# Key slots 128 bytes longer, and the third pair's stacked weights loaded and split half a pair sooner

## The chip, the core and the metric

The kernel runs on one core of one Trainium2 chip. The metric is the device time of one execution in microseconds (us). Before the change it is 1113.81 us, the median of three runs (1112.98 to 1114.1).

## What is computed

A transformer block in float32 on one sequence of 2048 rows of 576 numbers: a layer norm, then windowed attention (32 heads of 18 numbers, eight keys at a distance of two rows) and, in parallel, a squared-ReLU layer with 4608 hidden units. Cut to what matters:

```python
def _A_ref(x, wqkv, wo):
    q, k, v = split(x @ wqkv)
    idx = pos[:, None] - arange(8)[None] * 2
    logits = einsum("bhsd,bhswd->bhsw", q, k[idx]) * 18 ** -0.5
    attn = softmax(where(idx >= 0, logits, -1e9))
    return einsum("bhsw,bhswd->bhsd", attn, v[idx]) @ wo

def _B_ref(x, w1, b1, w2, b2):
    r = relu(x @ w1 + b1)
    return (r * r) @ w2 + b2

xn = layernorm(x)
return x + _A_ref(xn, ...) + _B_ref(xn, ...)
```

## The kernel before

**Tiling.** The 2048 rows are four blocks of 512 (`b` = 0 to 3), taken in two halves (`s` = 0: blocks 0 and 1, `s` = 1: blocks 2 and 3). The 576 input rows of a product are four chunks of 128 and a rest of 64. The 4608 hidden units are 36 tiles of 128, taken two at a time as 18 pairs `p`. Every float32 operand is split into a high part that TensorE takes in one pass (ScalarE, ACT, rounds it) and a low part (VectorE, DVE, subtracts); a product is high by high plus the two mixed terms.

**One pair** (`ffn_pair`) multiplies two hidden tiles with two blocks by seven products of Strassen's kind (`T1`, `T3`, `B11`, `T2`, `B22`, `B21`, `T4`) instead of eight. A `product` is six matmuls of 128x128 by 128x512, and `work(0)` to `work(3)` put seven matmuls each of the second layer (line 533) between them. TensorE (PE) takes them in the order B11, T1, work(0), T2, work(1), T3, B21, work(2), B22, T4, work(3). In the first half the rest of 64 rows costs eight further matmuls for each pair (`left`, line 633), which makes 7 x 6 + 8 + 28 = 78. In the second half, from pair 2 on, the rest is **stacked**: one further matmul for each product takes high and low parts of the rest together, its weights from `LW[p % 2]` (a part of a tile named `w1r`) and its moving operand from `ST[...]` (tiles `x40`, `x41`, `x4d` and the second `w1r` tile). That makes 7 x 7 + 28 = 77.

**Where the stacked weights come from.** `load_left_weights(p)` (line 584) fetches 256 KB on the SP queue into the raw tile `LR["w"]`, named `mb`, of which there is one. `left_weight_sums` makes the Strassen sums in it (three DVE instructions). `left_weight_hi(p)` rounds it into `LW[p % 2]` on ACT (line 593). `left_weight_lo(p)` subtracts on DVE, and then issues the load for `p + 1` into the same raw tile. In the second half, pair 0 has the end of the attention projection of block 1 as its filler; pair 1 makes the stacks of the rest (`stack_sums`, `stack_hi`, `stack_lo`; tiles `kv` and `w1r`), and in its later part loads and splits the weights of pair 2, the third pair. From pair 2 on each pair prepares the weights of the next one (`ready`).

**Order.** Nothing is reordered: each engine and each DMA queue takes its instructions as the code issues them. DVE and ACT also carry the attention of later blocks, in pieces that `side(k)` issues one after the other. The raw weights of the second layer (`w2r`) are loaded on the same SP queue, each load as soon as DVE has taken the low part of the tile three before it.

**Memory.** Tiles of one name share slots in a pool, laid out one after the other in each partition. A key or value tile is 18 x 144 numbers, 10368 bytes, in three slots named `kv`; behind them lie `w1r`, `w2r`, `mb`, `pr`, `lg`, `r4`, `st`, some small tiles, `nm`, `xf`, `mr`, `mrt` and `q`. Ahead of them lie `h`, `X`, `x4`, `w1s`, `S` and `w2s`, from which nearly all matmuls read.

Of the kernel before, what the change touches and what calls it, by code (L numbers as in the profile page):

```python
# [8 lines left out]
F32 = mybir.dt.float32  # L9
# [7 lines left out]
P = 128  # L17
S, D, F = 2048, 576, 4608
# [3 lines left out]
NJ = TB // P  # L22
# [5 lines left out]
CG = HG * DH  # L28
QW = 3 * CG
HALO = (W - 1) * DIL  # L30
NE = HALO + NJ
# [14 lines left out]
def block_kernel(ctx: ExitStack, tc: tile.TileContext, x, xt, wqkv, wo, w1, b1, w2, b2, w1l, out):  # L46
# [3 lines left out]
    sb = ctx.enter_context(tc.tile_pool(name="sb", bufs=1))  # L50
# [6 lines left out]
    ov = out[:DM].rearrange("(c p) (b t) -> b p c t", p=P, b=NB)  # L57
    oe = out[DM:].rearrange("d (b t) -> b d t", b=NB)

    x0 = sb.tile([P, NJ, D], F32, name="kv", bufs=3)  # L60
    w0 = sb.tile([P, NC - 1, QW], F32, name="w1r", bufs=2)
    w4 = sb.tile([P, DE], F32, name="w2r", bufs=3)
    r0 = [w0[:, c] for c in range(NC - 1)] + [w4[:, :QW]]
# [33 lines left out]
    def flat(t, off, parts, n):  # L97
        a = t[0:1, 0:1]
        return bass.AP(tensor=a.tensor, offset=a.offset + off, ap=[parts, [1, n]])
# [4 lines left out]
    def tt(out, a, b, op):  # L104
        return nc.vector.tensor_tensor(out=out, in0=a, in1=b, op=op)  # L105
# [12 lines left out]
    X, x4, SS, xm, xf, mb = {}, {}, {}, {}, {}, {}  # L118
# [26 lines left out]
    def load_rows(b):  # L145
        rows_of[b] = sb.tile([P, NJ, D], F32, name="kv", bufs=3)
        nc.sync.dma_start(rows_of[b], xv[b])
# [194 lines left out]
    loads, landed, queue, free, lane, kept_back = [], {}, [], [0], [nc.sync], [0]  # L342

    def fetch():
        while free[0] > kept_back[0] and loads:
            free[0] -= 1
            kind, b, g = loads.pop(0)
            if kind == "x":
                load_rows(b)
                landed["x", b] = True  # L350
                continue
            t = landed[kind, b, g] = sb.tile([P, NE, CG], F32, name="kv", bufs=3)
            if kind == "k":
                q = landed["q", b, g] = sb.tile([P, NJ, CG], F32, name="q", bufs=2)
                lane[0].dma_start(q.rearrange("p j c -> p (j c)"),
                                  flat(scr["q"][g], (PAD + b * TB) * CG, [NJ * CG, P], NJ * CG))
            lane[0].dma_start(t.rearrange("p e c -> p (e c)"),
                              flat(scr[kind][g], (PAD + b * TB - HALO) * CG, [NJ * CG, P], NE * CG))

    def release():  # L360
        free[0] += 1
        fetch()
# [55 lines left out]
    def side(k, exp=True):  # L418

        while k > 0:  # L420
            if current[0] is None:
                if not queue or queue[0][0] not in landed:
                    return k
                name, make = queue.pop(0)
                current[:] = [make(), None, name]
            if current[1] == "exp" and not exp:
                return k
            try:
                current[1] = next(current[0])
                k -= 1  # L430
            except StopIteration:
                current[0] = None
        return 0
# [107 lines left out]
    ST, LW, LR = {}, {}, {}  # L541
    STACK = {T1: 0, T3: 1, B11: 2, T2: 3, B22: 4, B21: 5, T4: 6}

    def load_left_rows():
        t = LR["a"] = sb.tile([P, 4, TB], F32, name="w1r", bufs=2)
        nc.vector.memset(t[3 * L:], 0.0)
        for g in range(3):
            for k, b in enumerate((2, 3)):
                nc.sync.dma_start(t[g * L:(g + 1) * L, 2 * k:2 * k + 2], xlscr[b].rearrange("(q r) t -> r q t", q=2))

    def stack_sums():
        a, z = LR["a"], LR["s"]
        tt(z[:, 0], a[:, 2], a[:, 3], ALU.add)
        tt(z[:, 2], a[:, 0], a[:, 2], ALU.subtract)
        tt(z[:, 1], z[:, 0], a[:, 0], ALU.subtract)
        tt(z[:, 3], a[:, 1], z[:, 1], ALU.subtract)

    def stack_hi(to, v):
        nc.scalar.activation(to, v, AF.Copy)

    def stack_lo(to, v):
        rows = slice(L, 2 * L)
        tt(to[rows], v[rows], to[rows].bitcast(F32), ALU.subtract)

    def open_stacks():
        t = LR["st"] = sb.tile([P, 4, TB], F32R, name="w1r", bufs=2)
        for i, k in enumerate((B11, B21, T4, T1)):
            ST[k] = t[:, i]

    def one_stack(k, name):  # L570
        ST[k] = mt.tile([P, TB], F32R, name=name)
        stack_hi(ST[k], LR["s"][:, {T2: 1, T3: 2, B22: 3}[k]])

    def one_stack_lo(k):
        stack_lo(ST[k], LR["s"][:, {T2: 1, T3: 2, B22: 3}[k]])

    def open_left_weights():
        t = sb.tile([P, 2, 7, P], F32R, name="w1r", bufs=2)
        LR["w"] = sb.tile([P, 7, P], F32, name="mb")
        LW[0], LW[1] = t[:, 0], t[:, 1]  # L580

    def load_left_weights(p):
        if p < NP:
            nc.sync.dma_start(LR["w"][:, 2:6], w1l[p])

    def left_weight_sums():
        r = LR["w"]
        tt(r[:, 0:2], r[:, 3:5], r[:, 2:4], ALU.subtract)
        tt(r[:, 3], r[:, 4], r[:, 0], ALU.subtract)
        tt(r[:, 6], r[:, 5], r[:, 3], ALU.subtract)  # L590

    def left_weight_hi(p):
        nc.scalar.activation(LW[p % 2], LR["w"], AF.Copy)

    def left_weight_lo(p):
        rows = slice(2 * L, P)
        tt(LW[p % 2][rows], LR["w"][rows], LW[p % 2][rows].bitcast(F32), ALU.subtract)
        load_left_weights(p + 1)
# [4 lines left out]
    def ffn_pair(s, p, work, first=False):  # L603
        b0, b1 = 2 * s, 2 * s + 1
        n = s * NP + p
# [14 lines left out]
        def product(to, slot, a, start=False):  # L620
            mm = [(weight(slot, 0, c), a(0, c)) for c in range(2)]
            for c in range(2):
                mm += [(weight(slot, 1, c), a(0, c)), (weight(slot, 0, c), a(1, c))]
            if stacked:
                mm.append((LW[p % 2][:, STACK[slot]], ST[slot]))
            for i, (l, r) in enumerate(mm):
                nc.tensor.matmul(to, l, r, start=start and i == 0, stop=i == len(mm) - 1, skip_group_check=True)  # L627

        def left(to, f, v):
            if stacked:  # L630
                return
            for k in range(2):
                nc.tensor.matmul(to, weight(LEFT, k, f), v, start=False, stop=k == 1, skip_group_check=True)  # L633
# [35 lines left out]
        if s and p == 2:  # L669
# [3 lines left out]
            one_stack_lo(B22)  # L673
            release()
        if s and p == 1:
            stack_sums()
            open_stacks()
            stack_hi(LR["st"][:, 0:2], LR["a"][:, 0:2])
            stack_hi(ST[T4], LR["a"][:, 3])
# [53 lines left out]
        relu(r0[:, 0], ba, f0)  # L733
        if s and p == 1:
            open_left_weights()
            load_left_weights(2)
            stack_lo(ST[T1], LR["s"][:, 0])
            one_stack(T2, "x40")
        work(2)

        def third():
            product(bc, B22, S4)
            left(bc, 1, x4["d"])
            if s and p == 1:
                one_stack_lo(T2)
                left_weight_sums()
                left_weight_hi(2)
            elif not first:
                side(2)
            tt(r0[:, 1], bc, u[:, 0], ALU.add)  # L750
            relu(r0[:, 1], r0[:, 1], f1)
# [12 lines left out]
        else:  # L764
# [1 line left out]
            h0 = square_hi(r0)  # L766
            square(r0)
            fourth()
        if s and p == 1:
            left_weight_lo(2)  # L770
        side(2, False)
        hs[n] = h0
        prev["r"] = r0, r1, h0
# [310 lines left out]
    def phase_b0():  # L1084
        b = 1
# [119 lines left out]
        def filler(i):  # L1205
            if i < 2:
                quads(1, 1, [len(steps) - 2 + i])
            if i == 1:
                load_left_rows()
                for g in (2, 3):  # L1210
                    offer(2, g)
                for g in range(G):
                    offer(3, g)
            if i == 2:
                xr[b] = [mt.tile([P, NC - 1, TB], F32, name="h", bufs=3)]
                nc.sync.dma_start(xr[b][0], yscr)
                open_y(b)
                o_hi(b, 0), o_hi(b, 1)
                o_lo(b, 0), o_lo(b, 1)
            if i == 2.5:  # L1220
                o_hi(b, 2), o_hi(b, 3)
                chunks(0)
                o_lo(b, 2), o_lo(b, 3)
                chunks(1)
            if i == 3:
                open_left(b)
                nc.sync.dma_start(kept(b, NC - 1), yleft)
                o_hi(b, 4)
                o_lo(b, 4)
                next(prev["finish"])  # L1230
                chunks(2)
                side(1)
                chunks(3)
                w2_hi()
                add(b, o_ops(b, 4), range(NC))
                finish(b, False)
                w2_lo()
# [80 lines left out]
    def open_rows():  # L1318
# [23 lines left out]
            inverse_std(rs[j], ln[0, j][:, 1:2])  # L1342

        def minus_mean(j):
            nm = sb.tile([P, 1], F32, name="nm", bufs=2)
            nc.vector.tensor_scalar(out=nm, in0=ln[0, j][:, 0:1], scalar1=-1.0, scalar2=rs[j], op0=ALU.mult, op1=ALU.mult)
            return nm

# [88 lines left out]
        nm = minus_mean(2)  # L1437
# [19 lines left out]
        nm = minus_mean(3)  # L1457
# [161 lines left out]
```

## Time and profile before

The profiled execution took 1115.46 us, of which 1113.8 us is the span from the first to the last instruction; the rest lies around it.

| of the span of 1113.8 us | busy |
|---|---|
| PE (matmuls) | 1102.4 us, 99% |
| DVE | 912.0 us, 82% |
| ACT | 575.5 us, 52% |
| POOL | 115.2 us, 10% |
| DMA | 258 GB/s mean |

| stage | us from the span's start |
|---|---|
| queries, keys and values of blocks 0 and 1 | 0 to 112 |
| pairs of the first half | 112 to 410 |
| second layer of block 1 | 410 to 547 |
| queries, keys and values of blocks 2 and 3 | 547 to 621 |
| pair 0 of the second half, and the projection of block 1 | 621 to 652 |
| pair 1 | 652 to 670 |
| pairs 2 to 17 | 670 to 957 |
| second layer of block 3, and the end | 957 to 1114 |

Rows of a timeline give start, duration, engine, line, operation, output <- inputs, shape, and in brackets how long the engine was idle before and what ended that. Matmuls overlap, and a row's duration runs to the modelled end of its last one: the pace is read from one row's start to the next one's. Line 105 is a helper that every DVE operation on two tensors goes through, so such rows are told apart by their tiles.

### The profile page before, as it was taken

To read this page: it belongs to the slowest core of one execution; us is meant where nothing else is said; L and a number is where in the kernel's file an instruction comes from. 1 tells how busy PE (TensorE), PEld (TensorE's weight loads), DVE (VectorE), ACT (ScalarE), POOL (GpSimd) and SP (SyncE) were. 2 spreads that over 40 slices of the span, in tenths; PEclk is the share of its full clock that TensorE was granted. 3 is DMA by queue.
4 is the path that set the end of the run, shared out by engine and by line. 5 is a ranking of instruction groups with operands and counts; after the bars stand their busy time and mean duration, and the time that the engine had idled before them with its cause. 6 is when DMAs were issued, how large, how long until landed. Compare 5 with 4: busy or idle time off the path is not lost.

```text
span 1113.8 us, 13890 instructions
## 1 busy us (share of the span) xinstructions
PE 1102.4 (99%) x4950; PEld 926.3 (83%) x4950; DVE 912.0 (82%) x1223; ACT 575.5 (52%) x809; POOL 115.2 (10%) x219
## 2 busy tenths in 40 slices
PE   9999999999999999999999998999999999999998
PEld 7998888888888888888899886888888888888886
DVE  7696979897997979999979488978988788899654
ACT  5435765556566554456344355555555555533342
POOL 4000101020110100100010200202102021001100
PEclk9999999999999999999999999999999999999999
DMA  8957987889799686966855976768686685866762
GB/s 295 337 167 237 338 295 262 293 206 372 250 246 364 250 329 221 337 227 213 277 147 158 335 264 252 276 247 319 216 312 236 263 314 203 311 207 209 277 192 82
DMA packets 100279, 287.83 MB, mean 258 GB/s; under 512 B 13288, under 2 KB 41712, under 8 KB 85488
## 3 DMA queue, kind: packets, MB, share of 16 engines
q1 hardware_dynamic: 65280, 188.15, 49.1%
q0 software_dynamic: 10544, 52.14, 13.0%
q10 hardware_dynamic: 24384, 46.64, 12.3%
q8 instruction: 39, 0.64, 0.2%
q14 instruction: 32, 0.26, 0.1%
HBM read 205.14 MB, written 81.74 MB: 258 GB/s over the span
## 4 chain that ended last, share of the span: by engine, by line
PE 92%; DVE 3%; DMA 2%; ACT 1%; issue 1%; POOL 0%; ACTq 0%; SPq 0%; DVEq 0%; POOLq 0%
PE p L533 46%; PE p L627 31%; PE p L1041 6%; PE p L335 5%; PE p L633 3%; PE p L1045 1%; DMA w1s<-w 1%; DMA mb<-in_w1l 1%; PE p L1399 1%; DVE h L105 0%; DVE w1r L105 0%; DVE pr L105 0%; DVE w1s L105 0%; DVE w2s L105 0%; DMA kv<-in_x 0%
## 5 line engine op out<-in xcount | busy, mean ns | idle before, releaser
L533 PE MATMUL p<-h,w2s 128*128 128x512 f32 x2066 | 493.0, 390 | 0.2 <-ACT h L640 0.2
L533 PEld LDWEIGHTS p<-h,w2s 128*128 128x128 f32 x2066 | 387.9, 188 | 83.3 <-ACT h L640 0.6
L627 PE MATMUL p<-X,w1s 128*128 128x512 f32 x864 | 220.5, 390 | 0.8 <-DVE w1s L105 0.8
L627 PEld LDWEIGHTS p<-X,w1s 128*128 128x128 f32 x864 | 162.2, 188 | 36.0 <-DVE w1s L105 1.2
L506 ACT ACTIVATE w2s<-w2r 128x640 fp32r<-128x640 f32 x164 | 120.2, 735 | 114.9 <-PE p L533 89.2
L627 PE MATMUL p<-S,w1s 128*128 128x512 f32 x648 | 166.7, 393 | 0.6 <-ACT r L688 0.6
L105 DVE TENSOR_TENSOR w2s<-w2r,w2s 128x576 fp32r<-128x576 f32 x164 | 123.4, 754 | 40.5 <-ACT w2s L506 39.7
L627 PEld LDWEIGHTS p<-S,w1s 128*128 128x128 f32 x648 | 122.3, 189 | 27.2 <-ACT r L688 1.4
L412 POOL DMA_DIRECT2D o<-q x128 | 69.3, 607 | 584.4 <-DVE q L105 582.5
L636 ACT ACTIVATE r<-r,b1t 128x512 f32<-128x512 f32 x72 | 52.0, 722 | 124.9 <-DVE r L105 123.8
L384 DVE TENSOR_REDUCE lg<-pr 128x64 f32<-128x1152 f32 x64 | 86.5, 1352 | 1.5
L105 DVE TENSOR_TENSOR pr<-lg,kv 128x1152 f32<-128x1152 f32 x64 | 86.7, 1355 | 1.3
L105 DVE TENSOR_TENSOR pr<-q,kv 128x1152 f32<-128x1152 f32 x64 | 86.6, 1353 | 0.9
L105 DVE TENSOR_TENSOR pr<-pr 128x576 f32<-128x576 f32 (+1 forms) x128 | 77.5, 606 | 3.2
L644 ACT ACTIVATE r<-r 128x1024 f32<-128x1024 f32 x72 | 76.1, 1057 | 1.2
L105 DVE TENSOR_TENSOR h<-r,h 128x1024 fp32r<-128x1024 f32 (+3 forms) x46 | 51.8, 1136 | 26.6 <-ACT r L644 18.5
L105 DVE TENSOR_TENSOR r<-p,r 128x512 f32<-128x512 f32 (+1 forms) x77 | 53.0, 688 | 23.1 <-PE p L627 11.4
L105 DVE TENSOR_TENSOR w1s<-w1r,w1s 128x1024 fp32r<-128x1024 f32 (+1 forms) x42 | 50.3, 1198 | 16.5 <-ACT w1s L474 16.4
L688 ACT ACTIVATE r<-p 128x512 f32<-128x512 f32 x36 | 21.6, 599 | 72.8 <-PE p L627 72.4
L105 DVE TENSOR_TENSOR h<-h 128x1024 fp32r<-128x1024 f32 x36 | 43.9, 1221 | 5.4 <-ACT h L938 5.4
L636 ACT ACTIVATE r<-p,b1t 128x512 f32<-128x512 f32 x72 | 48.3, 672 | 0.0
L533 PE MATMUL p<-w1s,w2s 128*128 128x512 f32 x195 | 44.7, 389 | 0.0
(193 smaller groups left out, 1174.9 us busy)
## 6 DMA issues: line engine op xcount, KB each, us to landing
w2r<-in_w SPq DMA_DIRECT2D x144, 320.0 KB, 3.6
kv<-kvq POOLq DMA_DIRECT2D x29, 1296.0 KB, 9.6
w<-w1s SPq DMA_DIRECT2D x36, 1024.0 KB, 8.9
w1s<-w ACTq DMA_DIRECT2D x34, 1024.0 KB, 7.3
h<-r SPq DMA_DIRECT2D x36, 512.0 KB, 6.6
h<-h SPq DMA_DIRECT2D x36, 512.0 KB, 4.0
w1r<-in_w SPq DMA_DIRECT2D x18, 640.0 KB, 7.6
kvq<-st ACTq DMA_DIRECT2D x48, 216.0 KB, 3.8
```

The costliest lines, as they stand in the source:

```text
L105: return nc.vector.tensor_tensor(out=out, in0=a, in1=b, op=op)
L335: nc.tensor.matmul(p[:, :QW], l, r, start=k == 0, stop=k == len(mm) - 1)
L384: nc.vector.tensor_reduce(out=lg[:, j * HG:(j + 1) * HG].rearrange("p a w -> p w a"), in_=pr.rearrange("p w (a d) -> p w a d", d=DH), axis ...
L412: nc.gpsimd.dma_start(rows[:, i], q[i * L:(i + 1) * L, :, a:z])
L506: nc.scalar.activation(w2s[stream[i]][:, :DE], raw2[i], AF.Copy)
L533: nc.tensor.matmul(yp[b][c], v, a, start=c not in yb[b], stop=c in last and c not in [o[0] for o in ops[i + 1:]], skip_group_check=True)
L627: nc.tensor.matmul(to, l, r, start=start and i == 0, stop=i == len(mm) - 1, skip_group_check=True)
L633: nc.tensor.matmul(to, weight(LEFT, k, f), v, start=False, stop=k == 1, skip_group_check=True)
L636: nc.scalar.activation(to, a, AF.Relu, bias=b1t[:, f:f + 1])
L644: nc.scalar.activation(r, r, AF.Square)
L688: nc.scalar.activation(u[:, 0], bb, AF.Copy)
L1041: nc.tensor.matmul(to, l[:, js], r, start=start and n == 0, stop=n == len(mm) - 1, skip_group_check=True)
```

## The change

There are two parts.

**The load and the split of the third pair's stacked weights.** The raw tile `mb` is opened and its load issued in pair 0's filler, behind the loads of the rest's rows (`load_left_rows`), instead of in pair 1. The sums go ahead of `stack_sums` in pair 1, the high part to where the load was, and the low part behind product B22, with the load for pair 3 right after it.

**Addresses.** Key and value tiles get 32 more float32 at their end (128 bytes), so a slot is 10496 bytes instead of 10368; each of the two slots of `nm` is 32 floats instead of one. What is computed with them is the same. Where tiles start, modulo 256 bytes, in the memory maps of the two programs:

| tiles | before | after |
|---|---|---|
| `h`, `X`, `x40`, `x41`, `x4d`, `w1s`, `S`, `w2s` | 224 | 224 |
| `kv` (three slots) | 224, 96, 224 | 224, 224, 224 |
| `w1r`, `w2r`, `mb`, `pr`, `r4` | 96 | 224 |
| `xf` | 160 | 224 |
| `q` | 192 | 0 |

```diff
-    x0 = sb.tile([P, NJ, D], F32, name="kv", bufs=3)
+    def kv_tile(n):
+        return sb.tile([P, n], F32, name="kv", bufs=3)
+
+    x0 = kv_tile(NJ * D).rearrange("p (j d) -> p j d", d=D)
...
-            t = landed[kind, b, g] = sb.tile([P, NE, CG], F32, name="kv", bufs=3)
+            t = landed[kind, b, g] = kv_tile(NE * CG + 32)[:, :NE * CG].rearrange("p (e c) -> p e c", c=CG)
...
     def open_left_weights():
         t = sb.tile([P, 2, 7, P], F32R, name="w1r", bufs=2)
-        LR["w"] = sb.tile([P, 7, P], F32, name="mb")
         LW[0], LW[1] = t[:, 0], t[:, 1]
...
         if s and p == 1:
+            left_weight_sums()
             stack_sums()
...
             open_left_weights()
-            load_left_weights(2)
+            left_weight_hi(2)
             stack_lo(ST[T1], LR["s"][:, 0])
             one_stack(T2, "x40")
...
             if s and p == 1:
+                left_weight_lo(2)
                 one_stack_lo(T2)
-                left_weight_sums()
-                left_weight_hi(2)
...
-        if s and p == 1:
-            left_weight_lo(2)
         side(2, False)
...
                 load_left_rows()
+                LR["w"] = sb.tile([P, 7, P], F32, name="mb")
+                load_left_weights(2)
...
-            nm = sb.tile([P, 1], F32, name="nm", bufs=2)
+            nm = sb.tile([P, 32], F32, name="nm", bufs=2)[:, :1]
```

On DVE, from the split of a `w2s` tile in pair 1 to the first attention piece (`pr`) behind pair 1, before (`kv<-w1r` and its two neighbours are the stack sums, `mb<-mb` the sums of the stacked weights, `w1r<-mb` their low part, `r<-p,r` additions that free a PSUM bank):

```order
L105 TENSOR_TENSOR kv<-w1r 128x512 x2
L105 TENSOR_TENSOR kv<-kv,w1r 128x512
L105 TENSOR_TENSOR kv<-w1r,kv 128x512
...
L105 TENSOR_TENSOR r_5626<-p_5556,r_5596 128x512
L105 TENSOR_TENSOR w1r<-kv,w1r 32x512
L105 TENSOR_TENSOR x_5644<-kv,x_5644 32x512
L105 TENSOR_TENSOR mb<-mb 128x256
L105 TENSOR_TENSOR mb<-mb 128x128 x2
L105 TENSOR_TENSOR r_5625<-p_5556,r_5596 128x512
L105 TENSOR_TENSOR w1r<-mb,w1r 64x896
L105 TENSOR_TENSOR pr<-q,kv 128x1152
```

and after:

```order
L108 TENSOR_TENSOR mb<-mb 128x256
L108 TENSOR_TENSOR mb<-mb 128x128 x2
L108 TENSOR_TENSOR kv<-w1r 128x512 x2
L108 TENSOR_TENSOR kv<-kv,w1r 128x512
L108 TENSOR_TENSOR kv<-w1r,kv 128x512
...
L108 TENSOR_TENSOR r_5631<-p_5558,r_5601 128x512
L108 TENSOR_TENSOR w1r<-kv,w1r 32x512
L108 TENSOR_TENSOR w1r<-mb,w1r 64x896
L108 TENSOR_TENSOR x_5648<-kv,x_5648 32x512
L108 TENSOR_TENSOR r_5630<-p_5558,r_5601 128x512
L108 TENSOR_TENSOR pr<-q,kv 128x1152
```

The three sums moved ahead of the stack sums, and the low part ahead of the second `r<-p,r`, which no longer has the sums in front of it. On ACT, `w1r<-mb` (line 593) changes places with the copy of one stack that stood ahead of it.

On the SP queue, from the loads of the rest's rows on, before:

```order
L549 DMA w1r<-xl_148 32x2x512
L1216 DMA h<-y_185 128x2048
...
L496 DMA w2r<-in_w 128x640 x2
L584 DMA mb<-in_w1l 128x512 x2
L654 DMA h_168<-r_5626 128x1024
```

and after:

```order
L552 DMA w1r<-xl_148 32x2x512
L586 DMA mb<-in_w1l 128x512
L1218 DMA h<-y_185 128x2048
...
L499 DMA w2r<-in_w 128x640 x2
L586 DMA mb<-in_w1l 128x512
L656 DMA h_168<-r_5631 128x1024
```

The first of two loads of `mb` moved ahead of the load of `h`, past nine loads and four stores; the second stays where it was. PE's and POOL's instructions keep their order.

## The prediction

> **What bounds the kernel now.** I read the page first, its busy times and its chain of waits:
>
> ```profile
> PE 1102.4 (99%) x4950; PEld 926.3 (83%) x4950; DVE 912.0 (82%) x1223; ACT 575.5 (52%) x809; POOL 115.2 (10%) x219
> PE 92%; DVE 3%; DMA 2%; ACT 1%; issue 1%; POOL 0%; ACTq 0%; SPq 0%; DVEq 0%; POOLq 0%
> ```
>
> TensorE sets the end. No matmul is added or removed, so time can come only from PE's waits, from its clock, and from the pace at which matmuls follow each other. The view of waits names the one long wait inside the program:
>
> ```profile
> PE p L627 <- DVE w1r L105: 2.9, 1, 2.9
> ```
>
> The timeline at the border of pairs 1 and 2 shows what led to it, and windows its clock (columns: stretch, length, then busy time of PE, PEld, DVE, ACT, POOL, granted clock, DMA share, GB/s):
>
> ```profile
> 631.47 5.79 SPq L549 DMA_DIRECT2D w1r<-xl  x6
> 657.30 1.28 DVE L105 TENSOR_TENSOR kv<-w1r 128x512 f32<-128x512 f32 x2
> 664.51 0.69 DVE L105 TENSOR_TENSOR r<-p,r 128x512 f32<-128x512 f32 x1
> 664.89 10.48 SPq L584 DMA_DIRECT2D mb<-in_w1l  x2
> 665.24 0.73 ACT L636 ACTIVATE r<-r,b1t 128x512 f32<-128x512 f32 x1 [2.61 <-DVE r L105]
> 665.25 1.23 PEld L627 LDWEIGHTS p<-X,w1s 128*128 128x128 f32 x6 [0.29 <-DVE r L105]
> 670.60 1.52 PE L627 MATMUL p<-X,w1s 128*128 128x512 f32 x6
> 671.78 1.08 DVE L105 TENSOR_TENSOR mb<-mb 128x256 f32<-128x256 f32 x3 [4.01 <-DMA mb<-in_w1l]
> 672.78 0.68 DVE L105 TENSOR_TENSOR r<-p,r 128x512 f32<-128x512 f32 x1
> 672.95 0.95 ACT L593 ACTIVATE w1r<-mb 128x896 fp32r<-128x896 f32 x1 [5.89 <-DVE mb L105]
> 673.93 1.09 DVE L105 TENSOR_TENSOR w1r<-mb,w1r 64x896 fp32r<-64x896 f32 x1 [0.46 <-ACT w1r L593]
> 675.05 1.36 DVE L105 TENSOR_TENSOR pr<-q,kv 128x1152 f32<-128x1152 f32 x1
> 675.07 0.79 PE L627 MATMUL p<-w1r 128*128 128x512 f32 x1 [2.95 <-DVE w1r L105]
> 678.53 1.76 PE L533 MATMUL p<-h,w2s 128*128 128x512 f32 x7
> 682.17 0.42 ACT L393 ACTIVATE lg<-lg 128x256 f32<-128x256 f32 x1 [2.30 <-DVE lg L105]
> 683.76 1.66 PE L627 MATMUL p<-S,w1s 128*128 128x512 f32 x6 [0.28 <-ACT r L688]
> ```
>
> ```profile
> 671.73:675.07 3.34, 0.39 (x2) 0.00 (x1) 2.72 (x6) 2.09 (x3) 0.00 (x0) 0.98 0.00 0
> 675.07:678.53 3.46, 3.46 (x8) 2.75 (x9) 3.43 (x3) 3.40 (x5) 0.54 (x1) 0.52 0.47 148
> ```
>
> The weights arrive at 671.8, DVE sums them, ACT rounds, DVE takes the low part until 675.02, and PE's seventh matmul of pair 2 goes at 675.07. Then the granted clock is 0.52 for 3.46 us.
>
> For the pace I take the chain in order of time, where PE waits for nothing: two pairs of the first half, then pairs of the second.
>
> ```profile
> 146.19 2.72 PE p L627 x12
> 148.91 1.59 PE p L533 x7
> 163.87 2.72 PE p L627 x12
> 701.77 3.20 PE p L627 x14
> 704.97 1.62 PE p L533 x7
> 949.48 3.20 PE p L627 x14
> 957.51 2.54 PE p L533 x11
> ```
>
> 12 matmuls in 2.72 us and 7 in 1.59 are 227 ns each. A pair of the first half takes 163.87 - 146.19 = 17.68 us for 78 matmuls, 226.7 ns each. A pair of the second half takes (949.48 - 701.77) / 14 = 17.69 us for 77, 229.8 ns each: the matmul that stacking saves is given back by pace.
>
> **The load and split: what the wait costs.** At 227 ns, work(0) would start 14 matmuls behind 670.60, at 673.78; it starts at 678.53. The wait and the half clock behind it cost 4.75 us (3.1 us of standing, 1.65 us of slow matmuls). Then T3 would follow behind work(0), T2 and work(1), 21 matmuls behind 678.53, at 683.3. It starts at 683.76, because the copy of T2 stands on ACT behind the exponential, which waits for DVE: 0.45 us, and 0.1 us more at its first matmuls.
>
> **What takes its place.** The load now goes out behind the loads of the rest's rows, at 631.47 + 5.79 = 637.3, and its sums need it at 657.3: hidden. The three sums (1.08 us) go ahead of the stack sums, into a stretch where DVE has no gap:
>
> ```profile
> 652.92:665.20 12.28, 12.28 (x55) 9.96 (x54) 12.12 (x18) 5.14 (x8) 0.00 (x0) 1.00 0.92 309
> ```
>
> Queued behind them are the stack sums, two `w2s` splits, the stack splits and the `r<-p,r` of 664.51, for which PE waits before B22. That wait, 0.29 us on the weight side now, grows by the whole 1.08. A pause of 1.2 us is a third of the one that brought the half clock, so I price no clock for it. In the new order ACT rounds the weights behind its two relus, at about 667.5 to 668.5 (now: relus from 665.24, moved by 1.08). DVE takes the low part (1.09) until 669.6, the stack part until 670.2 and the second `r<-p,r` (0.68) until 670.9. PE wants the weights at 670.60 + 1.08 + 1.36 = 673.0: they are ready 3.4 us before. The added ACT and DVE times there (0.95 and 1.09) lie in gaps of 5.89 and 4.01 us in the rows above.
>
> **What is late next.** DVE's chain to T3 (attention, low part of `h`, sums for pair 3, two stack splits, maximum, exponential on ACT, copy of T2) starts at `pr`, now 675.05, then 670.85: 4.2 us earlier, so T3 may start at 679.56. PE gets there at 683.76 - 4.75 - 0.45 + 1.08 = 679.64. The two nearly tie, and T3's wait goes. The sums for pair 3 need their load, issued at about 669.6, by 674.85.
>
> ```profile
> DMA to landing us min/median/max: 2.6/6.9/11.2
> ```
>
> Of 16 such loads the fastest landed in 2.6 us and the median in 6.9. The engines moved nothing from 671.73 to 675.07, so I take some 3 us and no wait; at 6.9 it would land at 676.5, 1.65 us late. Sum of this part: -4.75 - 0.55 + 1.08 = **-4.2 us**, bounds -2.5 (the late load) and -4.75 (half of the 1.08 absorbed).
>
> **Addresses.** Nothing in the trace shows a 128-byte step by itself, so I look for what differs between matmuls that run at 227 ns and those that do not.
>
> ```profile
> L627 PE MATMUL p<-w1r x64: 393/393/794, 675.1 to 957.1; 128*128 128x512 f32 x64
> L627 PE MATMUL p<-x,w1r x32: 397/397/397, 681.5 to 950.7; 128*128 128x512 f32 x32
> L533 PE MATMUL p<-xf,w2s x9: 394/394/394, 650.6 to 652.5; 128*128 128x512 f32 x9
> L533 PE MATMUL p<-w1s,w2s 128*128 128x512 f32 x195 | 44.7, 389 | 0.0
> ```
>
> Those on `w1r` (weights, or both operands) and those on `xf` show 393 to 397 ns, and all nine of `xf` 394. Their twins on `w1s`, the same operation on the same weights, show 389. `w1r` and `xf` are the tiles of 512-column matmuls that do not start at 224 modulo 256, and after the change they do. Matmuls behind a `w1r` one run slow too: the seven of 704.97 take 1.62 us, not 1.59. If the start is the cause, the second half goes to 226.7 ns: 77 x 3.1 = 0.24 us a pair, over (957.51 - 683.76) / 17.69 = 15.5 pairs 3.7 us, and 0.05 for `xf`. Bounds: 0, and -3.8. It might also be the place far back in the partition, which stays; but 432-column matmuls that read `r4` (short `r` in the rows), further back still, show what those on `h` show (by line and form: busy us, mean ns):
>
> ```profile
> L1041 PE MATMUL p<-h,X 128*128 128x432 f32 x144 | 32.1, 358 | 0.0
> L1041 PE MATMUL p<-r,X 128*128 128x432 f32 x48 | 10.2, 359 | 0.0
> ```
>
> That leaves the start. I take **-3.75 us**.
>
> A rule speaks against this term. The Trainium skill (SBUF — State Buffer, Who interferes with whom) says that PE and ACT never wait on anyone at their ports, and its section on operand start alignment speaks of legality alone. By it the term is 0 and the sum -4.2; no run here shows yet which holds.
>
> For DVE the step costs nothing by these rows: the `kv` slots already start 128 bytes apart modulo 256, and 64 instructions on them agree within 1%.
>
> ```profile
> L105 DVE TENSOR_TENSOR pr<-q,kv x64: 1347/1352/1361, 53.1 to 1014.0; 128x1152 f32<-128x1152 f32 x64
> ```
>
> **Sum.** -4.2 - 3.75 = -7.95 us. The profiled execution took 1115.46 (span 1113.8), which gives 1107.5; the median of the runs, 1113.81, lies 1.65 below it. That is what the half clock cost, so the runs may lack it and gain that much less (again 1107.5), or the difference has nothing to do with it (1105.9). I take **1106.6**, with a range of its own of 1105.3 to 1108.
>
> **Rivals.**
>
> *The addresses change nothing.* Only the wait goes: 1109.6 by the median, 1111.3 with the half clock missing from it, middle 1110.4. For it: matmuls on `h` and `w2s` run slow behind `w1r` although both start at 224. Against: nine equal `xf` rows. This is also what the Trainium skill's SBUF page would have.
>
> *A new wait takes the place of the old.* Pair 3's weights land after 6.9 us, the exponential and T3 come 1.65 us later: 1108.2 with the address term, 1112 without. For it the median landing; against it the idle DMA engines.
>
> *Slower: the shifted tiles cost DVE.* `w1r`, `w2r`, `pr`, `r4` and `q` all move, and DVE is the next fullest engine:
>
> ```profile
> 701.77:719.46 17.69, 17.69 (x78) 14.47 (x78) 15.82 (x18) 9.68 (x13) 5.99 (x11) 1.00 0.71 246
> ```
>
> It decides from 12% longer DVE instructions on, where 15.82 passes 17.69. At 15% a pair takes 18.2 us; every second of 33 pairs is as full, so 16 x 0.5 = 8 us: 1118. Against it stand the even `kv` rows.
>
> *It doesn't do what it says*: DVE reaches the low part no earlier, because ACT's rounding is held by something else in its queue, and PE waits as before: 1113.8, or 1110.1 with the address term.
>
> **How the numbers follow.** Both terms 0.60, the wait alone 0.23, a new wait 0.08, slower 0.05, no effect 0.04. The range, 1104.8 to 1111.2, holds the first, nearly all of the second and half of the third. About 0.2% (2.2 us) is what a measurement of this kernel can tell from no change: 0.88 faster, 0.07 within (no effect, and the parts of the second and third nearest to 1112), 0.05 slower.
>
> **What would show it.** PE's wait on `w1r` at the start of pair 2 is gone, and no half clock follows. The weight side waits about 1.4 us for `r<-p,r` before B22. T3 of pair 2 starts close to 679.6. Seven `w2s` matmuls in pairs take 1.59 us, `w1r` and `xf` rows show 389 ns, and pairs of the second half take 17.45 us. I am wrong if pairs stay at 17.69, if the pause before B22 brings the half clock, or if PE waits at T3 for more than a microsecond.

## The result, and the profile after

The changed kernel takes 1107.54 us (median of five runs, 1106.94 to 1108.04) against 1114.1 us before (1112.98 to 1115.76): a ratio of 0.994, 95% interval 0.9926 to 0.9955. That lies in the range, 0.9 us above the value predicted. The profiled execution after has a span of 1106.2 us, 7.6 us under the one before.

The waits of TensorE in the view of waits (engine, line, releaser, then us in total, times, longest), one row from before and then three from after:

```profile
PE p L627 <- ACT r L688: 0.6, 2, 0.3
...
PE p L1318 <- DVE lg L1311: 2.1, 1, 2.1
PE p L629 <- ACT r L691: 1.5, 2, 0.8
PE p L629 <- DVE r L108: 0.9, 1, 0.9
```

The wait of 2.9 us for `w1r` is gone. Two others have grown: for `r<-p,r` ahead of B22 of pair 1 (line 108 is the helper that was 105), and for the copy of T2 ahead of T3 of pair 2 (ACT, 688 before and 691 after; 0.28 us before, 0.70 after). The other wait in that row lies in pair 0; it was 0.29 us before and is 0.85 here, but 0.49 in another profile of the change (e12), and it stands ahead of all that is compared below. The wait at the kernel's start (line 1318) is as before. The timeline after, at the same places as in the prediction:

```profile
657.08 1.07 DVE L108 TENSOR_TENSOR mb<-mb 128x256 f32<-128x256 f32 x3
...
666.02 1.23 PEld L629 LDWEIGHTS p<-X,w1s 128*128 128x128 f32 x6 [1.35 <-DVE r L108]
...
668.17 1.09 DVE L108 TENSOR_TENSOR w1r<-mb,w1r 64x896 fp32r<-64x896 f32 x1 [1.50 <-ACT w1r L595]
...
669.29 0.33 SPq L586 DMA_DIRECT2D mb<-in_w1l  x1
...
670.01 0.69 DVE L108 TENSOR_TENSOR r<-p,r 128x512 f32<-128x512 f32 x1
...
670.62 1.35 DVE L108 TENSOR_TENSOR pr<-q,kv 128x1152 f32<-128x1152 f32 x1
...
672.72 0.39 PE L629 MATMUL p<-w1r 128*128 128x512 f32 x1
...
673.68 1.23 DVE L108 TENSOR_TENSOR h<-r,h 128x1024 fp32r<-128x1024 f32 x1 [0.33 <-ACT r L646]
...
676.12 1.52 PE L629 MATMUL p<-S,w1s 128*128 128x512 f32 x6
...
676.35 0.68 DVE L108 TENSOR_TENSOR x<-kv,x 32x512 fp32r<-32x512 f32 x1 [0.46 <-ACT x L562]
...
680.16 1.66 PE L629 MATMUL p<-S,w1s 128*128 128x512 f32 x6 [0.70 <-ACT r L691]
```

The sums stand in DVE's full stretch, B22 starts late, the first stacked matmul goes at 672.72 with nothing to wait for, and T3 of pair 2 waits again. Two windows, of before and of after, cut this part at the last `xf` matmul, at the start of B22 of pair 1 and at the start of T3 of pair 2:

```profile
652.51:665.26 12.75, 12.75 (x58) 10.33 (x56) 12.55 (x19) 5.17 (x9) 0.00 (x0) 1.00 0.91 307
665.26:683.76 18.50, 15.27 (x60) 11.87 (x59) 12.00 (x20) 10.22 (x16) 1.07 (x2) 0.91 0.59 216
```

```profile
652.24:666.02 13.78, 12.85 (x58) 10.33 (x56) 13.52 (x22) 5.19 (x9) 0.00 (x0) 1.00 0.92 316
666.02:680.16 14.14, 13.44 (x59) 10.80 (x59) 11.07 (x17) 10.24 (x16) 1.07 (x2) 1.00 0.70 254
```

The first stretch is 1.03 us longer, the second 4.36 shorter: 31.25 us became 27.92, which is 3.33 us of the gain. The granted clock stays at 1.00. Nearly all of the rest of the gain is pace, as the chain in order of time and the views of the two tiles after show:

```profile
697.93 3.17 PE p L629 x14
701.11 1.59 PE p L536 x7
...
942.28 3.17 PE p L629 x14
```

```profile
L629 PE MATMUL p<-w1r x64: 389/389/389, 672.7 to 949.8; 128*128 128x512 f32 x64
L629 PE MATMUL p<-x,w1r x32: 389/389/389, 677.5 to 943.5; 128*128 128x512 f32 x32
L536 PE MATMUL p<-xf,w2s x9: 389/389/389, 650.4 to 652.2; 128*128 128x512 f32 x9
```

A pair of the second half takes (942.28 - 697.93) / 14 = 17.45 us, and all rows on `w1r` and `xf` show 389 ns.

### The profile page after: what moved, and what is told of

Same layout as the page of the kernel before. It is cut to its first block, busy times and chain, and to the rows that moved or that the text cites. A ratio compares the mean times of both kernels' runs of the same rounds, so it can differ in the third digit from the quotient of the medians.

```text
span 1106.2 us, 13892 instructions
## 1 busy us (share of the span) xinstructions
PE 1096.8 (99%) x4950; PEld 925.2 (84%) x4950; DVE 912.0 (82%) x1223; ACT 575.0 (52%) x809; POOL 115.4 (10%) x219
## 4 chain that ended last, share of the span: by engine, by line
PE 89%; DVE 5%; DMA 3%; ACT 1%; issue 1%; ACTq 0%; POOL 0%; DVEq 0%; POOLq 0%; SPq 0%
PE p L536 46%; PE p L629 31%; PE p L1041 5%; PE p L635 3%; DMA kvq<-st 2%; PE p L338 1%; PE p L1401 1%; PE p L1045 1%; DVE pr L108 1%; DMA kv<-kvq 1%; DVE lg L387 1%; DVE w1r L108 1%; DVE r L108 0%; PE p L1318 0%; DVE h L108 0%
```

## The experiments

Each ran on the same chip as runs of the kernel before; ratios are to that kernel's runs there. Two numbers from each trace carry the comparison: the stretch from the start of the last `xf` matmul to T3 of pair 2 (the part that the load and split concern), and from there to the start of the last matmul of the form `p<-x,w1r` (15 pairs, the part that pace concerns).

| kernel | to T3 of pair 2, us | pairs behind it, us | time, us | ratio to before, 95% interval |
|---|---|---|---|---|
| before | 31.25 | 266.92 | 1115.52 and 1115.09 | |
| the change | 27.92 | 263.32 | 1107.54 | 0.994 (0.9926 to 0.9955) |
| e1 addresses alone | 30.38 | 263.36 | 1110.96 | 0.9961 (0.9948 to 0.9975) |
| e2 load and split alone | 27.87 | 266.94 | 1111.89 | 0.9971 (0.996 to 0.9981) |
| e3 load early, split late | 27.32 | 263.33 | 1107.9 | 0.9935 (0.9923 to 0.9948) |
| e4 sums out of both chains | 27.10 | 263.71 | 1107.8 | 0.9933 (0.992 to 0.9945) |
| e5 the change again | 27.94 | 263.34 | 1108.45 | 0.9938 (0.9926 to 0.9951) |
| e6 both waits out | 26.30 | 264.14 | 1107.34 | 0.9929 (0.9917 to 0.9942) |
| e7 all starts at 0 | 27.94 | 263.31 | 1107.89 | 0.9935 (0.9922 to 0.9949) |
| e8 slots 256 longer | 27.88 | 266.90 | 1111.09 | 0.9967 (0.9957 to 0.9977) |
| e9 exponential later | 26.25 | 263.16 | 1106.49 | 0.9922 (0.9908 to 0.9936) |
| e10 gap of 128 bytes | 27.92 | 263.36 | 1107.48 | 0.9931 (0.9916 to 0.9946) |
| e11 clock kept up | 31.41 | 266.93 | 1115.0 | 1.0002 (0.9993 to 1.001) |
| e12 the change beside e9 to e11 | 27.92 | 263.36 | 1107.44 | 0.9932 (0.992 to 0.9945) |

Times of one kernel move by 1 us and more between runs; the two stretches repeat within 0.1 us over three profiles of the change. So the stretches decide, and the times confirm where they can.

### e1 and e2: the two parts of the change apart

e1 is the kernel before with the slots of `kv` and `nm` longer; e2 is the change with both as before:

```diff
-            t = landed[kind, b, g] = kv_tile(NE * CG + 32)[:, :NE * CG].rearrange("p (e c) -> p e c", c=CG)
+            t = landed[kind, b, g] = kv_tile(NE * CG).rearrange("p (e c) -> p e c", c=CG)
-            nm = sb.tile([P, 32], F32, name="nm", bufs=2)[:, :1]
+            nm = sb.tile([P, 1], F32, name="nm", bufs=2)
```

> The kernel before with the longer key slots and the longer nm slots alone. If the start of w1r and xf modulo 256 bytes sets the pace: w1r and xf matmuls show 389 ns instead of 393 to 397, pairs 3 to 17 of the second half take 17.45 us instead of 17.69, PE still waits 2.9 us at the first stacked matmul of pair 2, and the time falls by 3.75 us, to about 1110.3 against 1114.1. If the addresses do nothing: pairs stay at 17.69 and the time at 1114.1.

> The changed kernel with key slots and nm slots as before. If the two parts add up: no wait at the first stacked matmul of pair 2 and no half clock, pairs 3 to 17 stay at 17.69 us, T3 of pair 2 starts 3.6 us earlier than the 683.8 of before, and the time is 1114.1 - 3.7 = 1110.4. If the earlier weights were what brought the even pace: pairs at 17.45 us here too, and 1107.5.

The parts are separate. In e1 the pairs take what they take in the change and a wait for `w1r` remains (2.0 us here, 2.9 expected). In e2 that wait is gone and the pairs take what they took before. The tile view of e1, then of e2:

```profile
L630 PE MATMUL p<-w1r x64: 389/389/628, 675.8 to 954.2; 128*128 128x512 f32 x64
L630 PE MATMUL p<-x,w1r x32: 389/389/397, 682.3 to 947.9; 128*128 128x512 f32 x32
```

```profile
L629 PE MATMUL p<-w1r x64: 393/393/398, 672.1 to 952.9; 128*128 128x512 f32 x64
L629 PE MATMUL p<-x,w1r x32: 390/397/397, 677.0 to 946.5; 128*128 128x512 f32 x32
```

Medians fall by 4.6 us and 3.6 us. The sum, 8.2, is more than the 6.6 to 7.7 that the change itself gives beside the same kernel. The stretches add up: 3.56 in e1's pairs and 3.38 in e2's way to T3, against 3.33 + 3.60 in the change. e1's way to T3 is shorter too, by 0.87 us: its sums, which wait for the load, start 18.41 us behind the last `xf` matmul, and 19.28 us before. That may be the rest.

### e8, e10, e7: what it is about the addresses

e8 makes key slots 256 bytes longer, so `w1r` and `xf` lie further back still, but at 96 modulo 256. e10 leaves the key slots as before and puts an unused 128 bytes between them and `w1r`. e7 moves every tile from `h` on by 224 bytes, to 0 modulo 256. The three edits, in this order:

```diff
-            t = landed[kind, b, g] = kv_tile(NE * CG + 32)[:, :NE * CG].rearrange("p (e c) -> p e c", c=CG)
+            t = landed[kind, b, g] = kv_tile(NE * CG + 64)[:, :NE * CG].rearrange("p (e c) -> p e c", c=CG)
```

```diff
-            t = landed[kind, b, g] = kv_tile(NE * CG + 32)[:, :NE * CG].rearrange("p (e c) -> p e c", c=CG)
+            t = landed[kind, b, g] = kv_tile(NE * CG)[:, :NE * CG].rearrange("p (e c) -> p e c", c=CG)
+    sb.tile([P, 32], F32, name="gap")
     w0 = sb.tile([P, NC - 1, QW], F32, name="w1r", bufs=2)
```

```diff
-    b2t = const.tile([P, 64], F32, name="b2t")[:, :NC]
+    b2t = const.tile([P, 8], F32, name="b2t")[:, :NC]
```

> The changed kernel with key slots 256 instead of 128 bytes longer: everything behind them lies 384 bytes further back than in the changed kernel, and w1r and xf start at 96 modulo 256, as w1r did before. If the start modulo 256 sets the pace: w1r matmuls show 393 to 397 ns, pairs 17.69 us, 3.7 us over the changed kernel. If it is the place in the partition, or any shift away from the old one helps: 17.45 us and no difference.

> The changed kernel with key slots as before and one unused tile of 128 bytes between them and w1r, so that w1r and xf start at 224 modulo 256 as in the changed kernel, but at 480 instead of 224 modulo 512, and the key slots stay where they were before. If 256 is the period and the key slots have no part in it: 389 ns and 17.45 us a pair, time as the changed kernel. If the period is 512 or more: 393 to 397 ns, 17.69 us a pair, 3.7 us more.

> The changed kernel with b2t padded to 8 floats instead of 64, so that everything from h on lies 224 bytes further ahead and all tiles that matmuls read start at 0 modulo 256. If it is equality between the tiles that counts: pace and time as in the changed kernel, 17.45 us a pair. If 224 itself counts: w1r, h, X and S matmuls of both halves show 393 to 397 ns, 2% more in all stages of 512 columns, 15 us more.

The tile views of e8, of e10 and of e7:

```profile
L629 PE MATMUL p<-x,w1r x32: 390/397/397, 677.5 to 947.0; 128*128 128x512 f32 x32
L536 PE MATMUL p<-xf,w2s x9: 387/395/398, 650.3 to 652.2; 128*128 128x512 f32 x9
```

```profile
L630 PE MATMUL p<-x,w1r x32: 389/389/393, 677.6 to 943.6; 128*128 128x512 f32 x32
L537 PE MATMUL p<-xf,w2s x9: 389/389/389, 650.5 to 652.3; 128*128 128x512 f32 x9
```

```profile
L629 PE MATMUL p<-x,w1r x32: 389/389/389, 677.1 to 943.1; 128*128 128x512 f32 x32
L536 PE MATMUL p<-xf,w2s x9: 389/389/389, 650.1 to 651.9; 128*128 128x512 f32 x9
```

Moved 384 bytes past the change's place, the slow rows are back, and 3.6 us of the pairs with them (266.90 against 263.34 in e5; the medians differ by 2.6 us, where 3.7 was expected). So it is neither the place far back in the partition nor any move away from the old one. The key slots have no part in it; 480 modulo 512 does as well as 224; and 0 does as well as 224, as long as the tiles of the 512-column matmuls share it. In the table, the ten rows in which `w1r` starts level with `X`, `S` and `w1s` modulo 256 take 263.2 to 264.1 us for the pairs, and the four in which it starts at 96 take 266.9. The simplest reading is that the tiles have to agree. It is not fully shown: no run puts all tiles at 96 or at 160, so these two starts could be slow by themselves. Why a tile out of step costs, and why matmuls behind it run slow too, the runs don't show.

### e5 and e12: the change again

> The changed kernel itself, beside the next three on one chip. Both theories: 6.5 us under the kernel before; pairs 3 to 17 at 17.45 us; 0.9 us of wait before B22 of pair 1 and 0.7 at T3 of pair 2.

> The changed kernel itself, as the measure for e9 and e10 on the same chip: 6.6 us under the kernel before.

Both repeat the first profile's stretches: 1108.45 and 1107.44 us beside 1115.09 and 1115.09. That is 6.6 us under the kernel before, as expected, and 7.7 us, one more.

### e11: what the half clock cost

The kernel before, with 26 bf16 matmuls of zeros added into the sum where PE waits for the weights, to keep the clock up:

```diff
+            if stacked and p == 2 and slot == B11:
+                for i, (l, r) in enumerate(mm):
+                    nc.tensor.matmul(to, l, r, start=start and i == 0, stop=False, skip_group_check=True)
+                for i in range(26):
+                    nc.tensor.matmul(to[:, :P], blank["z"], blank["z"], start=False, stop=False, skip_group_check=True)
+                mm, start = [], False
```

> The kernel before, with 26 small bf16 matmuls of zeros (128 columns) added ahead of the first stacked matmul of pair 2, where PE waits for the weights: PE stays busy through the 3 us wait. If T3 of pair 2 is released by the chain of DVE and ACT whatever PE does: no half clock, T3 still starts 18.5 us behind B22 of pair 1, PE waits about 2 us there instead of 0.45, and the time is that of the kernel before within 0.5 us. If the half clock counted in full in the time: 1.65 us less than before.

Windows of e11 (the partly filled wait, the stretch behind it, and the wait at T3 of pair 2), and rows of its timeline, T3 the last:

```profile
671.55:674.83 3.28, 1.63 (x28) 1.46 (x27) 2.72 (x6) 2.10 (x3) 0.00 (x0) 1.00 0.00 0
674.83:678.41 3.58, 3.58 (x15) 2.93 (x16) 3.54 (x3) 3.52 (x5) 0.54 (x1) 1.00 0.44 134
681.38:683.51 2.13, 0.39 (x3) 0.00 (x1) 1.54 (x5) 1.58 (x4) 0.43 (x1) 1.00 0.96 343
```

```profile
671.55 1.63 PE L628 MATMUL p<-blank 128*128 128x128 bf16 x26
674.83 0.50 PE L633 MATMUL p<-w1r 128*128 128x512 f32 x1 [1.65 <-DVE w1r L105]
...
683.51 1.67 PE L633 MATMUL p<-S,w1s 128*128 128x512 f32 x6 [1.74 <-ACT r L694]
```

The added matmuls take 1.63 us, so they fill half of the wait only, and PE still stands for 1.65 us. That was enough: the granted clock is 1.00 where it was 0.52, and PE stands still at T3 instead, 1.74 us. T3 starts 31.41 us behind the last `xf` matmul, 31.25 before. The time does not move. The half clock ran in the shadow of another chain: what it cost was time that PE would have waited at T3.

### e3, e4, e6, e9: the chain that holds T3

e3 moves only the load, and leaves sums, high and low part where they were. e4 takes the sums for pair 2 into pair 0, and those for pair 3 behind the subtraction of the maximum. e6 takes the sums for pair 2 into pair 0 and puts the exponential of pair 2 behind the copy of T2. e9 is e6 with the next attention piece later. The core of e6 and e9:

```diff
                 o_hi(b, 4)
+                left_weight_sums()
                 o_lo(b, 4)
...
-        if not first:
+        if s and p == 2:
+            side(1, False)
+        elif not first:
             side(1 if p == 1 else 3 if s else 2 + p % 2, s == 1)
...
         nc.scalar.activation(u[:, 0], bb, AF.Copy)
+        if s and p == 2:
+            side(2, True)     # e9: side(1, True), and side(3, False) at the pair's end
```

> The changed kernel, but only the load of the third pair's weights goes early; sums, high and low part stand where they stood before the change. If DVE's chain to the exponential decides when T3 of pair 2 starts: the wait before B22 shrinks from 1.35 to 0.3 us, PE waits about 1.8 instead of 0.7 us at T3, and the time is that of the change, 1107.5 within 0.3. If the 1.08 us of sums ahead of B22 count in full: 1106.5. If the late low part still holds PE at the first stacked matmul of pair 2: a wait there of some tenths, and over 1107.5.

> The changed kernel with the sums for pair 2 made in pair 0, ahead of DVE's full stretch, and the sums for pair 3 made behind the subtraction of the maximum, out of the chain to the exponential. If these two chains are what is left of the wait: 0.3 us before B22 instead of 1.35, T3 of pair 2 starts near 678.1 instead of 680.2 with no wait over 0.3 us, and the time is 1107.5 - 2 = 1105.5. If T3 is held by something else than DVE's chain: 1106.5 at best, with a wait at T3 of about 1.7 us.

> The changed kernel with the sums for pair 2 made in pair 0, and in pair 2 the exponential issued behind the copy of T2. If ACT's chain (relu, two squares, relu, copy, square, two stack copies, and the exponential that waits for DVE) is what holds T3: no wait over 0.2 us before B22 and at T3, the stretch from the last xf matmul to T3 of pair 2 falls from 27.9 to 25.9 us, and the time is 2 us under the changed kernel. If the copy of T2 then waits for something else: T3's wait stays near 0.7 us and 1 us is gained.

> As e6 (sums for pair 2 in pair 0, the exponential of pair 2 behind the copy of T2), and the first piece of attention values behind the exponential moves from before to behind the addition that PE waits for at B22 of pair 2. If that 1.36 us piece is what made e6 wait 0.83 us at B22 of pair 2: no wait over 0.3 us from B22 of pair 1 to T3 of pair 3, and 2.6 us under the changed kernel on the same chip. If DVE's other work there is enough to hold it: the wait stays over 0.5 us, and 1.8 us is gained.

The second `r<-p,r` of pair 1 starts what follows. From its start to T3 of pair 2 it is 683.76 - 672.78 = 10.98 us before, and 10.98 in e1 and e11 and 10.97 in e3, where the low part (1.09 us) also stands between `r<-p,r` and `pr`. It is 680.16 - 670.01 = 10.15 us in the change, and 10.15 in e2 and e4, where the low part stands ahead. So in these kernels T3 follows that addition at a distance that the place of the low part sets, whatever PE does.

e3 takes the wait before B22 away, as expected, and its T3 comes 0.60 us earlier than in the change, not at the same time (PE waits 1.07 us there, not 1.8): I had left out that `r<-p,r` comes earlier too. In e4, where 2 us were expected, sums out of the front bring 0.82 us; sums out of the back bring nothing, since DVE then waits for ACT's copies of the stacks:

```profile
677.24 0.68 DVE L108 TENSOR_TENSOR x<-kv,x 32x512 fp32r<-32x512 f32 x1 [1.44 <-ACT x L562]
681.05 1.65 PE L629 MATMUL p<-S,w1s 128*128 128x512 f32 x6 [0.70 <-ACT r L694]
```

In e6 the wait at T3 is gone and the stretch to it is 26.30 us (25.9 expected), but B22 of pair 2 starts 0.83 us late, since `r<-p,r` now stands behind an attention piece: the pairs behind it take 264.14 us. The median is 1.1 us under the change's in e5, not 2. In e9 that piece is moved, and from B22 of pair 1 to T3 of pair 3 nothing is late but that first B22, by 0.3 us:

```profile
651.81:664.74 12.93, 12.82 (x58) 10.29 (x56) 12.74 (x20) 5.17 (x9) 0.00 (x0) 1.00 0.90 297
664.74:678.02 13.28, 13.28 (x58) 10.99 (x59) 10.29 (x15) 10.60 (x16) 1.07 (x2) 1.00 0.81 279
```

Its two stretches are 1.87 us shorter than the change's on the same chip (26.25 + 263.16 against 27.92 + 263.36), less than the 2.6 expected, which had counted e6's 0.83 as a gain over the change. Its median is 0.95 us lower, 1106.49 against 1107.44: the lowest median of all. All four of its runs (1105.70 to 1106.99) lie under all five of the change's (1107.21 to 1107.91), so the sign holds on this chip; its size is no surer than that of other medians here.

## Why the prediction was right, and where not

**What bounds the kernel: right.** TensorE is busy 99% of the span before and after, and all gains are its waits and its pace.

**Addresses, -3.75 us: right.** The pairs gave 3.60, the nine `xf` matmuls show 5 ns less each, and from the last `p<-x,w1r` matmul to the program's last matmul it is 158.36 us before and 158.25 after, 0.1. The argument from twins (the same operation on the same weights from another tile) was enough to find the cause. The argument against a place far back was not: `r4` started at 96 too, and the mean of its 48 matmuls on `X` is 359 ns before and 358 after, so at 432 columns neither place nor start shows and these rows can't tell the two apart. e8 settled that. The Trainium skill (SBUF — State Buffer, Who interferes with whom) says that PE never waits on anyone; the forecast of 0 drawn from that for this term did not come true, with 393 to 397 ns against 389. That does not make the sentence wrong: whether a port is what these matmuls wait for, no run here shows.

**The load and split, -4.2 us: right in sign, 0.9 too much; 3.33 measured.** Three steps stand behind the difference.

- *The wait and the half clock cost 4.75 us.* Not as a price. They ran beside a chain that held T3 at 683.76 anyway, and e11 removes the half clock and half of the wait for nothing. The sum came near only because that chain was followed too, and the later of the two decided.
- *T3's wait goes; T3 starts at 679.64.* It started at 680.16 and PE's wait there grew. The step that failed is the chain moved as a block: I took 8.71 us from `pr` to T3, as before. It is 680.16 - 670.62 = 9.54. The low part had stood between `r<-p,r` and `pr` and gave ACT time for its relus and squares; with it ahead, DVE reaches `pr` early and waits for ACT later (0.33 us ahead of `h<-r,h` and 0.46 ahead of `x<-kv,x`, which is nearly all of the 0.83 added). The distance to hold on to was from `r<-p,r`.
- *The sums delay B22 by 1.08 us, and no clock falls.* Right: 1.03.

**The load for pair 3: right.** It landed in 2.4 us, not in the median 6.9, and the DMA engines had little else to move (a mean share of 0.34 from 669.29 to 671.70, this load included):

```profile
mb<-in_w1l SPq DMA_DIRECT2D x1, 256.0 KB, 2.4
```

By my rows the sums needed it at 670.85 + (678.85 - 675.05) = 674.65, not at the 674.85 that I wrote; they ran at 674.82.

**The basis of the sum: half wrong.** I held it possible that the 1.65 us between the profiled execution and the median before was the half clock, and moved the forecast up by 0.7 for it. e11 shows that the half clock costs no time. The runs of the kernel before beside the experiments say the same: 9 of 40 have a mean granted clock of 1.000, the rest 0.997 to 0.999, and chip by chip the median of the former is only 0.1 to 0.7 us the lower (1115.07 against 1115.73 at most). From the median alone the same sum gives 1105.9; with 3.33 in place of 4.2 it gives 1106.7, beside 1107.54. So the forecast came close partly by luck: the 0.7 added for the half clock and the 0.9 too much from load and split nearly cancel.

**The rivals.** "The addresses change nothing" is out by e1. The late load did not come; its place, T3 of pair 2, was the right one to watch, but ACT held it. Of longer DVE instructions nothing is seen: DVE is busy 912.0 us in both profiles.

## What to carry to other kernels

Where two twins of one matmul differ by a few nanoseconds, compare where their tiles start: here the tiles of the 512-column matmuls ran fastest where they agreed modulo 256 bytes, for 0.3% of the time. Before a wait and what follows it are priced at full length, look for the next point where the engine meets another chain, and take only the distance that this point moves; measure that distance from the last instruction that both chains share. A piece moved out of one chain shortens it only until the next engine in it becomes the longer limb.

## What the runs showed of the hardware

The pace of float32 matmuls of 512 columns is 226.7 ns from start to start when all tiles share their start modulo 256 bytes, and 229.8 on average over a pair in which 7 of 77 read `w1r` at another one. Matmuls on other tiles run slow behind some of those, and it matters which operand is out of step. Four rows from before, first with the weights alone in `w1r` (moving operand `x40`), then with the moving operand in it too:

```profile
947.49 0.40 PE L627 MATMUL p<-x,w1r 128*128 128x512 f32 x1
947.73 1.75 PE L533 MATMUL p<-h,w2s 128*128 128x512 f32 x7
...
952.28 0.39 PE L627 MATMUL p<-w1r 128*128 128x512 f32 x1
952.51 1.79 PE L533 MATMUL p<-h,w2s 128*128 128x512 f32 x7
```

Behind the first, the seven `w2s` matmuls show 389 ns each; behind the second, 387 to 398. A stop of PE has a like effect without any tile out of step: in the change, the six matmuls of T3 of pair 2 take 1.66 us behind their wait of 0.70 us, and behind the first of them they start 229 to 235 ns apart; the six at 676.12 take 1.52 us.

The half clock need not fall on the wait that brings it. In e1 PE waits 2.0 us up to 675.81, runs 1.5 us at full clock, and is then at half for 3.4 us:

```profile
673.44:675.81 2.37, 0.39 (x2) 0.00 (x0) 1.88 (x4) 2.09 (x3) 0.00 (x0) 1.00 0.00 0
675.81:677.31 1.50, 1.50 (x7) 1.23 (x7) 1.47 (x2) 1.47 (x2) 0.00 (x0) 1.00 0.34 27
677.31:680.74 3.43, 3.43 (x10) 2.66 (x9) 3.33 (x6) 3.28 (x6) 0.54 (x1) 0.50 0.78 279
```

The Trainium skill (TensorE: Matmul & The Clock Gate, What's actually happening) tells of an activity window of some 3.4 us that runs free of the program. The length and the delay here agree with it. The waits that brought the half clock, 2.95 us before and 1.98 in e1, are both shorter than that window. The waits of 1.65 and 1.74 us in e11 brought none, nor did the shorter ones of the other profiles.
